# Steps 13 to 17 of a tuned linear-attention and MLP kernel in three batches, with earlier casts and reordered transfers

## Chip, cores, metric

One core of a Trainium2 chip. The metric is the device time of one execution in microseconds (us); lower is better. A ratio is the mean time of one kernel's runs over that of the other's of the same rounds, so it is not quite the ratio of the medians quoted beside it; the interval given with it is a 95% interval.

## The reference

A block-wise linear attention with decay (4 batches, 8 heads, 768 positions, head dimension 64) is followed by a two-layer MLP with a tanh-GELU (512 to 2048 to 512, no bias) on its 3072 output rows. Cut to what matters:

```python
for b in range(nb):                                   # blocks of 64 positions
    intra = (qb @ kb^T * Dmask) @ vb                  # Dmask: lam ** (i - j), causal
    out[:, :, sl] = intra + (qb * lam_pow) @ kv_state
    kv_state = lam_block * kv_state + (kb * rev_pow)^T @ vb
x = out.transpose(0, 2, 1, 3).reshape(B * S, H * D)
return gelu_tanh(x @ w_in) @ w_out
```

## The kernel before

The attention is cut into 24 steps (256 positions of 4 heads each). A step needs q, k and v loaded, cast to fp16 with their decay (q on VectorE, k on ScalarE, v on GpSimd), q and k transposed by DMA, and then, on TensorE, scores S, products with v (O or OK), state updates K, and products of the old state u. On VectorE PT is the masked S, and t the state; on GpSimd u is the state with its mask. The finished rows x of two steps feed the MLP. Its dense matmuls stand in a queue of pieces, `filler`, and `fill(n)` issues n of them between the attention's steps, so that TensorE always has work. Some pieces carry sums on VectorE behind them (`gs`; the MLP's second product is done with seven block products in place of eight).

```python
def prep_v(s):                                        # v of step s, on GpSimd
    tv = a16p.tile([P, 2, HH, D], FP16, tag="v16", name=f"v16_{s}")
    pin(nc.gpsimd.tensor_tensor(wide(tv[:]), ld32[s][2][:], decay(dv, s), ALU.mult))
    a16[s] = a16[s] + (tv,)
    ...                                               # loads of step s + 3 are issued here

def R(n, s, ahead=None):                              # one step: S of n, products of s
    scores(n); ...; products(n, s); causal(n)         # causal: PT = S * mask, on VectorE
    ...; update(n, 0)                                 # t on VectorE, u on GpSimd

def burst(ns, ss, *mix):                              # a batch: S of all ns, then O of ss, K of ns, u
    for n in ns: scores(n)
    ...
    for n in ns: causal(n)
    ...
    for n in ns: update(n, 0)

# which sums stand behind which piece (groups of 512 rows)
behind(9, 0, 4, (1, 2, 4, 3))                         # first halves, behind piece 9 of 16
for k, m in zip(..., (1, 2, 4, 3)):
    behind(n1 + k, 4, 8, (m,))                        # second halves

FILL = {8: (0, 2, 1, 2), ..., 12: (0, 2, 1, 3),
        13: (0, 2, 1, 3), 14: (0, 3, 1, 3), 15: (0, 2, 1, 3), 16: (0, 2, 1, 3), 17: (0, 3, 1, 3)}
for n, (a, b, c, d) in FILL.items():                  # one step at a time
    stage_t(n); fill(a)
    prep_qk(n + 2) if n == 8 else prep(n + 2)
    fill(b); R(n, n - 1); fill(c); U(n)               # U: second half of the update
    ...
burst((18, 19), (17,))                                # from here on: two at a time
```

All matmuls write to one pool of eight PSUM buffers, called banks here; a tile waits until the earlier tile of its bank has been read. `pin` keeps the program's order on each engine.

## Time and profile before

| | before |
|---|---|
| time, median of 3 runs | 199.89 us (199.67 to 200.28) |
| profiled span | 198.3 us |
| busy share PE / DVE / ACT / POOL | 97% / 77% / 62% / 37% |
| PE, 87.21 to 119.52 us (the stretch that is rewritten) | busy throughout |

PE is TensorE, DVE VectorE, ACT ScalarE, POOL GpSimd, SPq the queue that issues transfers. A line of a timeline has start and duration in us, engine, line of the source, operation, output and inputs, shapes, the number of like instructions in a row, and in brackets the idle time before it with what ended it. The lines of the kernel before that carry the argument stand in the prediction below.

### The profile page before, as it was taken

To read this page: it belongs to the slowest core of one execution; us is meant where nothing else is said; L and a number is where in the kernel's file an instruction comes from. 1 tells how busy PE (TensorE), PEld (TensorE's weight loads), DVE (VectorE), ACT (ScalarE), POOL (GpSimd) and SP (SyncE) were. 2 spreads that over 40 slices of the span, in tenths; PEclk is the share of its full clock that TensorE was granted. 3 is DMA by queue.
4 is the path that set the end of the run, shared out by engine and by line. 5 is a ranking of instruction groups with operands and counts; after the bars stand their busy time and mean duration, and the time that the engine had idled before them with its cause. 6 is when DMAs were issued, how large, how long until landed. Compare 5 with 4: busy or idle time off the path is not lost.

```text
span 198.3 us, 5936 instructions
## 1 busy us (share of the span) xinstructions
PE 191.9 (97%) x2437; PEld 139.7 (70%) x2439; DVE 151.8 (77%) x296; ACT 123.0 (62%) x251; POOL 73.6 (37%) x85
## 2 busy tenths in 40 slices
PE   8879999999999999999999999999999999999993
PEld 2546544456887888754588755578888888888883
DVE  4887722789989989949899378999678997588720
ACT  3673878466693675577745486754668835778321
POOL 6594223456456652436433565047002030002000
PEclk9999999999999999999999999999999999999999
DMA  6999999999999999999864999320211200020205
GB/s 171 291 324 386 386 386 387 292 289 295 293 297 257 217 293 215 210 317 219 226 142 104 271 286 214 106 56 0 53 37 72 105 9 0 0 108 1 106 3 212
DMA packets 61706, 37.86 MB, mean 191 GB/s; under 512 B 17520, under 2 KB 54640, under 8 KB 61680
## 3 DMA queue, kind: packets, MB, share of 16 engines
q1 hardware_dynamic: 61136, 37.23, 71.8%
q8 instruction: 19, 0.31, 0.7%
q10 hardware_dynamic: 544, 0.26, 0.5%
q14 instruction: 7, 0.06, 0.1%
HBM read 27.26 MB, written 6.29 MB: 169 GB/s over the span
## 4 chain that ended last, share of the span: by engine, by line
PE 88%; SPq 4%; DMA 4%; ACT 1%; issue 1%
PE Hps L529 24%; PE MX L606 17%; PE MY L606 9%; PE HX L698 7%; PE O2ps L544 7%; PE MW L606 4%; DMA wi<-in_moe_w_in_dram 4%; SPq L70 4%; PE HY L698 4%; PE S L327 3%; PE Hps L789 3%; PE OK L385 2%; PE HW L698 2%; PE OK L376 2%; PE Tps L298 1%; PE O L436 1%
## 5 line engine op out<-in xcount | busy, mean ns | idle before, releaser
L529 PE MATMUL Hps<-xT,w_in 128*128 128x512 f16 (+1 forms) x288 | 51.0, 332 | 0.0
L488 POOL TENSOR_TENSOR u<-t,lumask 128x256 f16<-128x256 f32 x40 | 29.6, 752 | 49.7 <-DVE t L481 34.1
L529 PEld LDWEIGHTS <-w_in 128*128 128x128 f16 x288 | 27.8, 98 | 18.8
L533 ACT ACTIVATE gT<-Hps 128x512 f16<-128x512 f32 x56 | 32.9, 597 | 10.3 <-PE Hps L529 9.8
L337 DVE TENSOR_TENSOR PT<-S,mask 128x512 f16<-128x512 f32 x48 | 30.5, 682 | 7.4 <-PE S L327 7.3
L606 PEld LDWEIGHTS <-gs 128*128 128x128 f16 x320 | 31.1, 98 | 4.0 <-DVE gs L576 0.4
L258 POOL TENSOR_TENSOR v<-v,dv 128x512 f16<-128x512 f32 x24 | 29.9, 1249 | 7.3 <-DMA v<-in_v_dram 6.9
L606 PEld LDWEIGHTS <-gT 128*128 128x128 f16 x240 | 23.2, 98 | 3.5 <-ACT gT L533 0.5
L606 PE MATMUL MX<-w_sum,gs 128*128 128x256 f16 x160 | 21.5, 273 | 0.0
L271 DVE TENSOR_TENSOR qk<-q,dq 128x512 f16<-128x512 f32 x23 | 19.1, 835 | 1.1 <-DMA q<-in_q_dram 1.0
L576 DVE TENSOR_TENSOR gs<-gT 128x1024 f16<-128x1024 f16 (+1 forms) x24 | 18.4, 772 | 1.6 <-ACT gT L533 1.6
L276 ACT ACTIVATE qk<-k 128x512 f16<-128x512 f32 x24 | 15.0, 626 | 6.9 <-DMA k<-in_k_dram 6.7
L651 POOL TENSOR_TENSOR o<-u,q 128x512 f32<-128x512 f32 (+1 forms) x5 | 5.4, 1082 | 37.2 <-ACT u L623 37.2
L462 ACT ACTIVATE xT<-OK 128x256 f16<-128x256 f32 x34 | 13.0, 454 | 6.3 <-PE OK L385 6.0
L544 PE MATMUL O2ps<-w_out,gT 128*128 128x512 f16 x64 | 14.6, 379 | 0.0
L698 PEld LDWEIGHTS <-ws 128*128 128x128 f16 x128 | 12.5, 98 | 1.8
L623 ACT ACTIVATE u<-MX 128x256 f32<-128x256 f32 x18 | 6.9, 384 | 10.1 <-PE MX L606 10.1
L481 DVE SCALAR_TENSOR_TENSOR t<-t,lamu,OK 128x64 f32<-128x64 f32 x48 | 11.0, 274 | 1.4 <-issue 0.5
L327 PEld LDWEIGHTS <-qkT 64*64 64x64 f16 x384 | 6.1, 106 | 7.1 <-issue 3.4
L544 PEld LDWEIGHTS <-gT 128*128 128x128 f16 x64 | 6.1, 98 | 6.6
L606 PE MATMUL MY<-w_out,gs 128*128 128x256 f16 x80 | 10.7, 273 | 0.0
L606 PE MATMUL MX<-w_sum,gT 128*128 128x256 f16 x80 | 10.4, 273 | 0.0
(95 smaller groups left out, 311.6 us busy)
## 6 DMA issues: line engine op xcount, KB each, us to landing
q<-in_q_dram SPq DMA_DIRECT2D x24, 256.0 KB, 5.0
k<-in_k_dram SPq DMA_DIRECT2D x24, 256.0 KB, 5.1
v<-in_v_dram SPq DMA_DIRECT2D x23, 256.0 KB, 5.4
out_dram<-o SPq DMA_DIRECT2D x17, 256.0 KB, 4.1
wo<-in_moe_w_out_dram SPq DMA_DIRECT2D x4, 1024.0 KB, 9.5
wi<-in_moe_w_in_dram SPq DMA_DIRECT2D x4, 512.0 KB, 8.0
wi<-in_moe_w_in_dram SPq DMA_DIRECT2D x2, 1024.0 KB, 12.7
out_dram<-o SPq DMA_DIRECT2D x3, 512.0 KB, 5.0
```

What stands on the lines that cost most here:

```text
L258: pin(nc.gpsimd.tensor_tensor(wide(tv[:]), ld32[s][2][:], decay(dv, s), ALU.mult))
L271: pin(q_eng.tensor_tensor(wide(tq), q32[:], decay(dq, s), ALU.mult))
L276: pin(nc.scalar.activation(out=wide(tk), in_=k32[:], func=AF.Copy))
L337: pin(nc.vector.tensor_tensor(t[:, hl].rearrange("p b c d -> p b (c d)"), Sps[:].rearrange("p b c d -> p b (c d)"), mask[:].unsqueeze(1).t ...
L462: pin(nc.scalar.activation(out=d, in_=o, func=AF.Copy))
L488: pin(nc.gpsimd.tensor_tensor(u[:], state[half][:].unsqueeze(2).to_broadcast([P, 2, 2, D]), lumask[:, 2 * half : 2 * half + 2, :].unsqueez ...
L529: pin(nc.tensor.matmul(by_block(Hps[:, i, :]), w_in16[:, c, f * P : (f + 1) * P], x(c), start=(c == 0), stop=(c == NC - 1)))
L533: pin(nc.scalar.activation(out=dst, in_=Hps[:], func=AF.Gelu_apprx_tanh))
L544: pin(nc.tensor.matmul(O2[tau][0][:], gT[:, f % HF, f // HF, tau * P : (tau + 1) * P], w_out16[:, f, :], start=(n == 0), stop=(n == NF - 1)))
L576: pin(nc.vector.tensor_tensor(g_rows(m, i), g_rows(a, i), g_rows(b, i), op))
L606: pin(nc.tensor.matmul(dst, lhsT, rhs, start=(opens and i == 0), stop=(closes and i == HF - 1), skip_group_check=True))
L698: pin(nc.tensor.matmul(dst[:, i, :], w_in_block(a, slice(c, c + 1), slice(f * P, f * P + P))[:, 0], x_block(b, slice(c, c + 1))[:, 0], sta ...
```

## The change

Intent: handle steps 13 and 14, and 15 and 16, as batches (step 17 stays alone), so that the small matmuls stand together more often, and take the casts and transfers that a batch needs early enough. By the words of its author: "Steps 13 to 17 in three batches; casts of 15 and 16 two and three products ahead, loads of 18 behind the transposition of 16".

```diff
-                whole = g == 3 or (g, T) == (4, 0)      # store of group 4 in one transfer
+                whole = g == 3
...
+        if n == 12:
+            prep_qk(15)
         fill(d)
...
+    cast_qk(16)
+    fill(2)
+    burst((13, 14), (12,))
+    transpose_dma(16)
+    fill(1)
+    U(13)
+    U(14)
+    prep_v(15)                 # with the loads of 18
+    prep_v(16)                 # with the loads of 19
+    fill(6)
+    burst((15, 16), (13, 14))
+    fill(1)
+    U(15)
+    U(16)
+    prep(17)
+    fill(8)
+    prep(18)
+    R(17, 15)
...                            # prep 19 to 21 and the w_in sums, between pieces
-    burst((18, 19), (17,))
+    burst((18, 19), (16, 17))
+    prep_v(21)
```

Cuts: the removed rows 13 to 17 of `FILL`, the split of `prep_qk` into `cast_qk` and `transpose_dma`, and a condition that keeps a batch closing an even step from queueing its group too soon.

More of the change, by code (lines that the diff above doesn't have):

```diff
@@ L266, in prep_qk, with cast_qk @@
     def prep_qk(s):
+        cast_qk(s)
+        transpose_dma(s)
+    def cast_qk(s):
         q32, k32, _ = ld32[s]
@@ L277, in prep_qk, with transpose_dma @@
         a16[s] = (tq, tk)
+        whole_qk[s] = tqk
+    whole_qk = {}
+    def transpose_dma(s):
+        tqk = whole_qk.pop(s)
         if s >= FIRST_DMA_T:
@@ L444, in burst @@
         g, i = group_of[sbg]
-        if i == len(groups[g]) - 1:
+        if ss[-1] % 2 == 1 and i == len(groups[g]) - 1:
             queue_group(g, *mix)
@@ L971 @@
     fill(2)
-    FILL = {8: (0, 2, 1, 2), 9: (2, 2, 1, 2), 10: (0, 1, 1, 3), 11: (0, 2, 1, 2), 12: (0, 2, 1, 3),
-            13: (0, 2, 1, 3), 14: (0, 3, 1, 3), 15: (0, 2, 1, 3), 16: (0, 2, 1, 3), 17: (0, 3, 1, 3)}
+    FILL = {8: (0, 2, 1, 2), 9: (2, 2, 1, 2), 10: (0, 1, 1, 3), 11: (0, 2, 1, 2), 12: (0, 2, 1, 3)}
     for n, (a, b, c, d) in FILL.items():
@@ L984 @@
             prep_v(n + 2)
-        if n == 17:
-            prep_qk(20)
-            fill(1)
-            prep_qk(21)
-            fill(1)
-            prep_v(20)
-            prep_v(21)
-            fill(1)
-        else:
-            fill(d)
-        if 8 < n < 17:
-            sum_win((n - 7) // 2, (n - 1) % 2, nc.vector)
-    burst((18, 19), (17,))
+        if n == 12:
+            prep_qk(15)
+        fill(d)
+        if n > 8:
+            sum_win((n - 7) // 2, (n - 1) % 2, nc.vector)
+    cast_qk(16)
[16 more added lines that the diff above has]
+    R(17, 15)
+    fill(1)
+    U(17)
+    fill(1)
+    sum_win(3, 0, nc.vector)
+    fill(2)
+    prep(19)
+    sum_win(3, 1, nc.vector)
+    fill(2)
+    sum_win(4, 0, nc.vector)
+    fill(2)
+    sum_win(4, 1, nc.vector)
+    fill(2)
+    prep_qk(20)
+    fill(1)
+    prep_qk(21)
+    prep_v(20)
+    fill(3)
+    burst((18, 19), (16, 17))
+    prep_v(21)
     fill(2)
```

## The prediction

> **What bounds the kernel now.** I read the page first, then the chain of waits, then the waits of TensorE alone, then the timelines of PE, DVE and POOL between 80 and 130 us, where the changed steps lie.
>
> ```profile
> PE 191.9 (97%) x2437; PEld 139.7 (70%) x2439; DVE 151.8 (77%) x296; ACT 123.0 (62%) x251; POOL 73.6 (37%) x85
> PE 88%; SPq 4%; DMA 4%; ACT 1%; issue 1%
> ```
>
> TensorE is busy for 97% of the span, and the chain that ended last is PE for 88%; the rest is the load at the start and the last store. The list of waits, cut to PE and to 86 to 127 us, is empty, and the window 87.21 to 119.52 us has PE busy 32.31 of 32.31 us. So in the stretch that is rewritten nothing is waited for: only the issue time of the matmuls counts, and the change can win only by making the small matmuls cheaper, or lose by making PE wait. How dear the small matmuls are shows in the PE timeline:
>
> ```profile
> 87.21 0.42 PE L327 MATMUL S<-qkT 64*64 64x128 f16 x16
> 87.91 0.28 PE L385 MATMUL OK<-qkT,u 128*128 128x128 f16 x2
> 88.03 6.21 PE L529 MATMUL Hps<-xT,w_in 128*128 128x512 f16 x28
> ...
> 118.15 0.64 PE L327 MATMUL S<-qkT 64*64 64x128 f16 x32
> 119.28 0.40 PE L436 MATMUL O<-qkT,u 128*128 128x128 f16 x4
> 119.52 7.07 PE L529 MATMUL Hps<-xT,w_in 128*128 128x512 f16 x32
> 126.52 0.64 PE L327 MATMUL S<-qkT 64*64 64x128 f16 x32
> 127.81 0.40 PE L436 MATMUL O<-qkT,u 128*128 128x128 f16 x4
> 128.05 2.75 PE L529 MATMUL Hps<-xT,w_in 128*128 128x512 f16 x12
> ```
>
> From the first S to the next dense matmul, a single step takes 0.82 us (87.21 to 88.03; two matmuls of u) or 0.93 us (four of u); a batch of two steps that closes one takes 1.37 us (118.15 to 119.52), and one that closes two 1.53 us (126.52 to 128.05). Dense pieces of four 128x512 matmuls take 0.875 us each (eight in 119.52 to 126.52).
>
> The second thing to see is how DVE and POOL hold each other up:
>
> ```profile
> 103.55 0.68 DVE L636 TENSOR_TENSOR o<-MW,m 128x512 f32<-128x512 f32 x1
> 104.15 0.79 DVE L576 TENSOR_TENSOR gs<-gT 128x1024 f16<-128x1024 f16 x1
> 104.86 1.53 DVE L151 TENSOR_TENSOR ws<-w_in,ws 128x1024 f16<-128x1024 f16 x1
> ```
> ```profile
> 104.35 1.49 POOL L258 TENSOR_TENSOR v<-v,dv 128x512 f16<-128x512 f32 x1
> 112.86 1.04 POOL L258 TENSOR_TENSOR v<-v,dv 128x512 f16<-128x512 f32 x1
> ```
> ```profile
> 122.94 0.74 DVE L576 TENSOR_TENSOR gs<-gT 128x1024 f16<-128x1024 f16 x1 [0.68 <-ACT gT L533]
> 123.71 0.98 DVE L576 TENSOR_TENSOR gs<-gs,gT 128x1024 f16<-128x1024 f16 x1
> ```
>
> A v product alone takes 1.04 us, a ws or gs sum alone 0.68. Beside each other they take turns: gs ends at 104.94; v, issued at 104.35, ends at 105.84, 0.90 after it; ws, issued at 104.86, ends at 106.39, 0.55 after v. PT and t, with one input from SBUF, are not held.
>
> **What the Trainium skill says.** "SBUF — State Buffer", section "SBUF: two separate sides": the port pair that VectorE and GpSimd share is an exclusive lock, taken by a GpSimd operation or by a VectorE operation with two SBUF inputs; the other blocks for the whole instruction. The trace agrees, with the 0.90 and 0.55 us above. "TensorE: Matmul & The Clock Gate", section "Part 3: Packing small matmuls — row/col tiling": matmuls on different tiles overlap, and all complete in order. The trace agrees with the first (32 S matmuls of 216 ns span 0.64 us), and the second is why a held matmul holds all PE work. "Perfetto Trace Analysis", section "Identifying the Most-Contended Engine", warns that matmul busy time is no measure of headroom; so I use start-to-start times, not the 97%.
>
> **The change part by part.**
>
> 1. *PE, saved.* The order of instructions shows the same 4870 PE rows. Before, the stretch holds steps 13 and 14 (0.82 each), 15, 16, 17 (0.94, 0.93, 0.93) and the batch of 18 and 19 (1.37): 5.81 us. After, it holds a batch 13+14 that closes 12: 1.37 less two u matmuls at 0.058 = 1.26; a batch 15+16 that closes 13 and 14: 1.53 plus two u (0.11) less 8 missing K matmuls (0.06) = 1.58; step 17 alone 0.93; the batch 18+19 that closes 16 and 17: 1.53 + four u (0.24) = 1.77. Sum 5.54, so 0.27 us less. Between groups and dense work each group also loses an overlap: the dense matmuls of the stretch, 64 of 216 ns and 112 of 109 ns, make 26.04 us, but 32.31 - 5.81 = 26.50 us pass, 0.077 per group of six. Two groups fewer save 0.15. Together **0.42 us**.
>
> 2. *Casts and transpositions.* The casts of 15 and 16 move to ACT and DVE time that was idle (DVE waits 2.43 us before 87.67). The transposition of 16 is queued when 12 is closed, about 88.5 us, and right behind that of 15, which landed at 92.4 before (86.73 + 5.66). The loads of 18 no longer stand between the two. It should land near 93.3; PE wants it at 94.9. No wait, no gain.
>
> 3. *The store of group 4* becomes two transfers instead of one, near 140 us; the queue is idle there. Nothing.
>
> 4. *DVE and POOL behind the first batch.* This is where I expect a new wait. Call the batch's first S time B = 87.21. The first batch of the kernel before is the template, with B = 118.15: four PT end at B+2.95, u products start at B+3.22 and end at B+3.84, 4.41, 4.98, and gs 1 is issued at B+4.8 (here 4.7: fewer u matmuls), once gelu 8 is done. Now POOL has v of 15 and v of 16 queued straight behind the four u. Taking turns: gs 1 behind u 3, B+5.53; u 4, B+6.00; gs 2, B+6.54; v15 B+7.44; gs 3 B+7.99; v16 B+8.89; gs 4 B+9.44. Only then come the PT of step 15 in DVE's order: B+9.36 to B+10.05. PE gets to the batch 15+16 after 1.26 + 7 x 0.875 = B+7.39, needs v16 at about B+8.43 (waits to 8.9), and would start the next dense matmul at 7.39 + 1.58 = B+8.97. But that one writes the PSUM bank which S of step 15 held: in the built program, its wait on DVE is 15 counts behind that of the first dense piece after batch 13+14, and these 15 end at the first PT of step 15. So PE waits to about B+10.1: **1.13 us lost**, the wait for v16 included in it.
>
> 5. *Behind that.* The transposition of 17 is issued near 101.3 and lands 3.1 us later (as the one at 99.78 did), 104.4; S of 17 comes at 105.1. Later batches: DVE's queue behind 18+19 has one v more (21), some 0.6 us; PT of 20 then meets its S just in time. No loss.
>
> Sum: 199.89 - 0.42 + 1.13 = 200.60.
>
> **Rivals.**
> - *A: no new wait, the saving alone: 199.5.* For it: the moves of casts and loads look made to keep PE fed, and had gs 1 been issued 0.3 us earlier (before u 3) one turn would fall before v16, and PT of 15 would be in time. Against: gs 1 waited for gelu in the template too, and that follows PE's own pace to 0.1 us.
> - *B: the wait is shorter, 0.3 to 0.7 us: 199.8 to 200.2.* It needs v16 or a sum to go out of turn. The trace shows no such case.
> - *C: a transposition late as well.* The one of 16 has 1.6 us of room, that of 17 has 0.7. If DMA is slower (6.5 us to landing, the longest in the view of qkT), S of 17 waits 2 to 3 us more, 202 to 203. The queue is nearly empty near 101 us, so I give it little.
> - *D: PE busy time falls by more, since batches have fewer switches.* The 1.37 and 1.53 us of existing batches bound that: no more than 0.1 us beyond part 1.
>
> **Range and chances.** I give the wait of part 4 two chances in three, A and B nearly all the rest. The sum is 200.6; weighed with A and B I name **200.4 us**, range **199.3 to 201.0**. The runs before scatter from 199.67 to 200.28, so the sign itself is near the noise. 2% is 4 us, far from any of these: faster 0.005, within 2% 0.985, slower 0.01.
>
> **What would show it.** Right: in the profile after, batches of about 1.26, 1.6 and 1.77 us where PE doesn't wait; gs sums lengthened to 1.0 to 1.5 us beside v of 15 and 16; the first PT of step 15 some 2 us behind its S; and on PE one gap near 1.1 us before the first dense matmul behind batch 15+16, put down to DVE PT, with a shorter one at the K matmuls put down to POOL v. Wrong: no gap of PE in 94 to 99 us (then A, near 199.5); a gap at S of 16 or 17 put down to a transposition (C); batch times far from these (part 1).

## The result, and the profile after

201.09 us median (200.69 to 201.81, six runs) against 199.88 us (199.67 to 200.28, six runs): ratio 1.0063, interval 1.0037 to 1.0089. Slower, but by less than 2%, and 0.09 us above the predicted range. The six times stand in two groups: 200.69, 200.70, 200.74, and 201.43, 201.74, 201.81. The profiled run, 201.74, is of the upper group.

From the page of the changed kernel (lines of the steps stand 10 higher than before; L337 is now S, L347 PT, L586 gs, L539 Hps; v stays at L258):

```profile
PE 191.9 (96%) x2437; PEld 140.2 (70%) x2439; DVE 153.9 (77%) x296; ACT 122.7 (61%) x251; POOL 74.9 (37%) x85
PE 77%; DMA 8%; DVE 6%; SPq 4%; ACT 3%; issue 1%; DVEq 0%; ACTq 0%
```

PE is as busy as before to the tenth, and the span grew from 198.3 to 199.9 us, so the difference appears as waiting (only roughly: the ends of matmuls are modelled). The chain now runs over DVE and a transfer as well. The waits of PE from 60 us on, which were none before:

```profile
PE MX L616 <- ACT gT L543: 0.8, 1, 0.8
PE Hps L539 <- DVE PT L347: 0.4, 1, 0.4
PE K L435 <- POOL v L258: 0.3, 1, 0.3
```

The second and third are the ones foretold. The timeline of PE through them:

```profile
88.05 0.64 PE L337 MATMUL S<-qkT 64*64 64x128 f16 x32
89.30 6.21 PE L539 MATMUL Hps<-xT,w_in 128*128 128x512 f16 x28
95.44 0.64 PE L337 MATMUL S<-qkT 64*64 64x128 f16 x32
...
97.00 0.31 PE L435 MATMUL K<-v,qk 64*64 64x64 f16 x8 [0.35 <-POOL v L258]
97.24 0.51 PE L446 MATMUL O<-qkT,u 128*128 128x128 f16 x6
98.15 3.61 PE L539 MATMUL Hps<-xT,w_in 128*128 128x512 f16 x16 [0.40 <-DVE PT L347]
```

With B = 88.05 (B is the first S of step 13), K of step 16 waits to B+8.95 (foretold 8.9) and the dense matmul to B+10.10 (foretold about 10.1). The two idle times in brackets make only 0.75 us, but from its first S to the dense matmul the batch takes 2.71 us, 1.10 more than the 1.61 us that it takes below without waits. Start-to-start times are the ones to go by. DVE and POOL in the same time:

```profile
92.72 0.85 DVE L586 TENSOR_TENSOR gs<-gT 128x1024 f16<-128x1024 f16 x1 [0.38 <-ACT gT L543]
93.61 0.99 DVE L586 TENSOR_TENSOR gs<-gs,gT 128x1024 f16<-128x1024 f16 x1
94.63 1.42 DVE L586 TENSOR_TENSOR gs<-gT,gs 128x1024 f16<-128x1024 f16 x1
95.97 1.53 DVE L586 TENSOR_TENSOR gs<-gT 128x1024 f16<-128x1024 f16 x1
97.42 2.47 DVE L347 TENSOR_TENSOR PT<-S,mask 128x512 f16<-128x512 f32 x4
```
```profile
91.27 2.77 POOL L498 TENSOR_TENSOR u<-t,lumask 128x256 f16<-128x256 f32 x4 [5.74 <-DVE t L488]
94.01 2.94 POOL L258 TENSOR_TENSOR v<-v,dv 128x512 f16<-128x512 f32 x2
```

The four sums take 0.85 to 1.53 us each, where one alone takes 0.68, and the two v products 2.94 us together, where one alone takes 1.04. They take turns, and the first PT of step 15 starts at B+9.37 (foretold 9.36), almost two us behind its S at B+7.39. Seen alone it takes 0.68 us, to 98.10, and the dense matmul that was waiting for it starts at 98.15.

The first wait in the list was not foretold. It lies at 60.85 us, far ahead of the change:

```profile
58.09 0.63 ACT L280 ACTIVATE qk<-k 128x512 f16<-128x512 f32 x1 [1.00 <-DMA k<-in_k_dram]
```
```profile
60.85 0.28 PE L616 MATMUL MX<-w_out,gT 128*128 128x256 f16 x1 [0.81 <-ACT gT L543]
```

A cast of k on ACT waited 1.00 us for its load, the gelus behind it came late, and PE waited for them. In the kernel before the same cast did not wait:

```profile
56.98 0.63 ACT L276 ACTIVATE qk<-k 128x512 f16<-128x512 f32 x1
```

Before the casts and transfers of step 15, the two programs are the same on every engine. The traces show the same instructions in the same order; addresses, which traces do not show, I compared in the programs. Nothing of the change that I can find would put this wait there, and the runs below support that: two further profiles of the changed kernel do not have it, and a second profile of the kernel before does.

Where the 1.6 us of the profiled runs lie, from the starts of S in the timelines of PE and the spans:

| us | before | after |
|---|---|---|
| start to S of 8 | 57.25 | 57.27 |
| S of 8 to S of 9 (shared part) | 7.34 | 8.16 |
| S of 9 to S of 13 | 22.62 | 22.62 |
| S of 13 to the dense matmul behind batch 18+19 | 32.31 | 32.94 |
| from there to S of 20 | 7.00 | 7.00 |
| S of 20 to the end | 71.78 | 71.88 |

### The profile page after: what moved, and what is told of

Its sections match the earlier page's. It is cut to its first block, busy times and chain, and to the rows that moved or that the text cites. A ratio compares the mean times of both kernels' runs of the same rounds, so it can differ in the third digit from the quotient of the medians.

```text
span 199.9 us, 5931 instructions
## 1 busy us (share of the span) xinstructions
PE 191.9 (96%) x2437; PEld 140.2 (70%) x2439; DVE 153.9 (77%) x296; ACT 122.7 (61%) x251; POOL 74.9 (37%) x85
## 4 chain that ended last, share of the span: by engine, by line
PE 77%; DMA 8%; DVE 6%; SPq 4%; ACT 3%; issue 1%; DVEq 0%; ACTq 0%
PE Hps L539 19%; PE MX L616 17%; PE MY L616 9%; PE HX L708 7%; PE O2ps L554 6%; PE MW L616 4%; DMA wi<-in_moe_w_in_dram 4%; SPq L70 4%; PE HY L708 4%; DMA k<-in_k_dram 3%; PE Hps L799 3%; PE S L337 2%; DVE gs L586 2%; PE HW L708 2%; DVE PT L347 2%; ACT gT L543 1%
## 5 line engine op out<-in xcount | busy, mean ns | idle before, releaser
L539 PE MATMUL Hps<-xT,w_in 128*128 128x512 f16 (+1 forms) x288 | 50.8, 332 | 0.4 <-DVE PT L347 0.4
L498 POOL TENSOR_TENSOR u<-t,lumask 128x256 f16<-128x256 f32 x40 | 30.2, 769 | 49.6 <-DVE t L491 28.8
L539 PEld LDWEIGHTS <-w_in 128*128 128x128 f16 x288 | 27.8, 98 | 19.6 <-issue 0.5
L347 DVE TENSOR_TENSOR PT<-S,mask 128x512 f16<-128x512 f32 x48 | 30.3, 680 | 5.9 <-PE S L337 5.9
L258 POOL TENSOR_TENSOR v<-v,dv 128x512 f16<-128x512 f32 x24 | 30.3, 1267 | 7.9 <-DMA v<-in_v_dram 7.6
L586 DVE TENSOR_TENSOR gs<-gT 128x1024 f16<-128x1024 f16 (+1 forms) x24 | 17.0, 714 | 2.7 <-ACT gT L543 2.7
L472 ACT ACTIVATE xT<-OK 128x256 f16<-128x256 f32 x26 | 9.9, 454 | 7.3 <-PE OK L395 7.3
L472 ACT ACTIVATE xT<-O 128x256 f16<-128x256 f32 x22 | 8.0, 459 | 6.4 <-PE O L446 5.6
L616 PE MATMUL MX<-w_out,gT 128*128 128x256 f16 x80 | 10.2, 273 | 0.9 <-ACT gT L543 0.8
L586 DVE TENSOR_TENSOR gs<-gs,gT 128x1024 f16<-128x1024 f16 (+1 forms) x12 | 10.6, 887 | 0.3
```

What stands on the lines that cost most here:

```text
L347: pin(nc.vector.tensor_tensor(t[:, hl].rearrange("p b c d -> p b (c d)"), Sps[:].rearrange("p b c d -> p b (c d)"), mask[:].unsqueeze(1).t ...
L472: pin(nc.scalar.activation(out=d, in_=o, func=AF.Copy))
L498: pin(nc.gpsimd.tensor_tensor(u[:], state[half][:].unsqueeze(2).to_broadcast([P, 2, 2, D]), lumask[:, 2 * half : 2 * half + 2, :].unsqueez ...
L539: pin(nc.tensor.matmul(by_block(Hps[:, i, :]), w_in16[:, c, f * P : (f + 1) * P], x(c), start=(c == 0), stop=(c == NC - 1)))
L586: pin(nc.vector.tensor_tensor(g_rows(m, i), g_rows(a, i), g_rows(b, i), op))
L616: pin(nc.tensor.matmul(dst, lhsT, rhs, start=(opens and i == 0), stop=(closes and i == HF - 1), skip_group_check=True))
```

## The experiments

Theory: the batches save PE 0.42 us, and the turns that gs sums and v products take cost it 1.13 us. Rivals: batches cost more than they look; v of 16 alone holds PE; transfers hold it. A second question came from the result: is the upper group of times a mark of the change (C2), or of a load that either kernel meets by chance (C1)? Kernels are compared only within the same rounds.

| run | median us (kernel) | median us (before) | ratio, interval | S13 to dense, us |
|---|---|---|---|---|
| e1_before_again | 200.05 | 199.96 | 1.0000, 0.9969 to 1.0030 | 32.31 |
| e1_after_again | 200.70 | 199.96 | 1.0030, 1.0005 to 1.0054 | 32.94 |
| e2_v_early | 199.67 | 199.96 | 0.9978, 0.9952 to 1.0003 | 31.85 |
| e3_two_sums_late | 200.27 | 199.96 | 1.0009, 0.9973 to 1.0044 | 31.93 |
| e4_before_k7_late | 199.87 | 199.85 | 0.9994, 0.9977 to 1.0011 | 32.31 |
| e4_best | 199.71 | 199.85 | 0.9995, 0.9974 to 1.0016 | 31.85 |
| e5_loads_first | 201.94 | 199.85 | 1.0123, 1.0079 to 1.0167 | 33.53 |
| e6_casts_late | 199.56 | 199.85 | 0.9988, 0.9965 to 1.0010 | 31.85 |
| e7_after_third | 200.71 | 199.84 | 1.0039, 1.0023 to 1.0056 | 32.94 |
| e7_after_k7_late | 200.72 | 199.84 | 1.0050, 1.0029 to 1.0071 | 32.93 |
| e7_v_early_again | 199.66 | 199.84 | 0.9989, 0.9969 to 1.0009 | 31.85 |
| e7_old_store | 199.42 | 199.84 | 0.9978, 0.9953 to 1.0002 | 31.85 |
| e8_before_k10_late | 200.32 | 200.10 | 1.0015, 0.9993 to 1.0037 | 32.31 |
| e8_after_k10_late | 200.74 | 200.10 | 1.0044, 1.0025 to 1.0064 | 32.93 |
| e8_best | 199.46 | 200.10 | 0.9967, 0.9953 to 0.9981 | 31.85 |

The last column, from the first S of step 13 to the dense matmul behind batch 18+19, comes out of one profile each and repeats to 0.01 us over profiles that share that stretch; the whole times of one run spread over 0.35 to 2.6 us. That makes it the sharper instrument for what the change did.

### The two kernels again

No edit.

> A control: the kernel before, word for word, timed against itself. All theories: ratio 1.000 within noise (interval about 0.997 to 1.003). It also shows how often the late load in the part that both kernels share (steps 5 to 8) costs time: the changed kernel's profile lost 0.84 us there, before step 13, although its instructions, addresses and waits are the same as before's up to that point, and its six times fell into two groups, near 200.7 and near 201.6. Theory C1 (chance of the loads, in either kernel): here too some of the runs are 0.6 to 1.0 us above the others. Theory C2 (the changed kernel is hit more often): these runs stay within 0.6 us of each other, 199.7 to 200.3.

> The changed kernel again. Main theory (0.42 us saved, 1.1 us lost at the first dense matmul behind batch 15+16): the runs that are not hit by the late load come out at 200.6 to 200.8 again, 0.6 to 0.9 us above before, and the distance from the first S of step 13 to the first dense matmul behind batch 18+19 is 32.9 us (before: 32.3). C1: the group near 201.6 is seen less often or as often as by chance, and in the control too. C2: again about half of the runs near 201.6.

> The changed kernel a third time, for its scatter and one more profile. Its first six times had three of 201.4 to 201.8, its second six one of 201.2, the others lie at 200.5 to 200.8. C1 (the late load hits either kernel by chance, about one run in six, as it did before: 4 of 34 runs over 0.6 us above the lowest group): none to two of six over 201.2, median 200.6 to 200.8. C2 (the changed kernel is hit more often): two to four of six over 201.2. In an unhit profile the first S of 13 to that of 20 takes 39.9 us again (before: 39.3).

Measured: the control gave 199.8 to 200.94, one of six 0.55 us above the next; the kernel before, run 11 times beside it, had two such (200.92 and 201.28). The changed kernel gave 200.54 to 201.16, then 200.59 to 200.99. The unchanged changed kernel ran 18 times: four were above 201.1, three of them in the first six. The kernel before ran 56 times, control included: five were above 200.5. (Counted alike, as times more than 0.6 us above the kernel's own median, it is three of 18 against five of 56.) So upper times belong to either kernel; C1's main point holds. The control's profile shows the cause at work in the kernel before: the same cast waits 0.8 us for k, PE 0.3 us for the gelu behind it, and S of 8 to S of 9 takes 7.53 us. For the profiled high run of the changed kernel this load is nearly the whole story: its span is 1.16 us longer than that of e7_after_third, and 1.03 us of this lie between S of 8 and S of 9 (8.16 against 7.13). Whether the changed kernel meets such times somewhat more often these counts do not decide: of its times above 201.1, three of six fell in the first call and one of twelve after it. The median of the 18 is 200.74 us.

### Moving what takes turns

> Changed kernel, but the v products of 15 and 16 stand on POOL ahead of the first batch, where it idles for 5.7 us; the loads of 18 and 19 stay where the change put them. Main theory (gs sums and v products take turns, so PT of 15 comes late): the sums end near B+7.0 (B: first S of step 13), PT of 15 starts within 0.6 us of its S, both waits of PE behind batch 15+16 vanish, 1.1 us less than the changed kernel, 0.3 to 0.5 us less than before: ratio to before 0.998 (unhit runs near 199.5). Rival (batches of two cost PE more than the profile of before tells, or ACT or DMA is the cause): PE still waits or the distance B to the dense matmul behind batch 18+19 stays over 32.5 us, ratio 1.003 or more.

> The changed kernel with v of 15 and 16 early, a second time: median 199.5 to 199.7, ratio to before 0.998 (first: 0.9978, 0.9952 to 1.0003), first S of 13 to that of 20 38.8 us. If the first result was luck: 0.999 or more.

```diff
+    def cast_v(s): ...             # the product alone
+    def load_behind(s): ...        # the loads of s + 3 alone
     cast_qk(16)
+    cast_v(15)
+    cast_v(16)
     fill(2)
     burst((13, 14), (12,))
...
-    prep_v(15)
-    prep_v(16)
+    load_behind(15)
+    load_behind(16)
```

```profile
93.41 0.69 DVE L592 TENSOR_TENSOR gs<-gT,gs 128x1024 f16<-128x1024 f16 x1
94.02 0.68 DVE L592 TENSOR_TENSOR gs<-gT 128x1024 f16<-128x1024 f16 x1
94.68 2.48 DVE L353 TENSOR_TENSOR PT<-S,mask 128x512 f16<-128x512 f32 x4
```
```profile
84.28 2.94 POOL L262 TENSOR_TENSOR v<-v,dv 128x512 f16<-128x512 f32 x2
90.05 2.77 POOL L504 TENSOR_TENSOR u<-t,lumask 128x256 f16<-128x256 f32 x4 [2.84 <-DVE t L494]
```
```profile
94.22 0.64 PE L343 MATMUL S<-qkT 64*64 64x128 f16 x32
95.48 0.51 PE L452 MATMUL O<-qkT,u 128*128 128x128 f16 x6
95.83 2.54 PE L545 MATMUL Hps<-xT,w_in 128*128 128x512 f16 x11
```

These are the timelines of DVE, POOL and PE. (In this kernel lines stand another 4 to 6 higher.) The v products now run at 84 us, behind step 12. The last two sums take 0.69 and 0.68 us, their time alone, and PT of 15 starts 0.46 us behind its S, as early as S lets it. PE has no wait at all from 60 us on, and the batch 15+16 takes 1.61 us (94.22 to 95.83; foretold 1.58). The stretch takes 31.85 us: 1.09 less than in the changed kernel (foretold 1.1) and 0.46 less than before (foretold 0.42). The sums end at B+7.87 (B is 86.83 here), not at the B+7.0 that I expected, because they still take turns with u; that is just in time. In time the gain over the kernel before is small: 0.9978 and 0.9989, and neither interval excludes 1.

> Changed kernel with its POOL order, but two of the four gs sums of the first half are put behind the cast of 17, so that PT of 15 and 16 stand in front of them on DVE. Main theory: v of 15 and 16 then meet at most one sum, v16 is ready near B+8.5 (PE wants it at B+8.4) and PT of 15 starts by B+7.9; PE's wait for PT vanishes, the one for v16 shrinks to 0.1 us or none; ratio to before 0.998 to 0.999. Rival (v16 alone holds PE, the sums do not matter): PE still waits 0.35 us for v16, ratio 1.003 or more. A new wait at MY, for the later sums, is possible on both.

```diff
-            behind(9, 0, 4, (1, 2, 4, 3))
+            if g == 3:
+                behind(9, 0, 4, (1, 2))
+                behind(13, 0, 4, (4, 3))
+            else:
+                behind(9, 0, 4, (1, 2, 4, 3))
```

Here POOL keeps the order of the changed kernel, and two sums step back on DVE, whose timeline shows:

```profile
92.70 0.98 DVE L586 TENSOR_TENSOR gs<-gs,gT 128x1024 f16<-128x1024 f16 x1
94.99 2.48 DVE L347 TENSOR_TENSOR PT<-S,mask 128x512 f16<-128x512 f32 x4 [1.31 <-PE S L337]
99.14 0.69 DVE L586 TENSOR_TENSOR gs<-gT,gs 128x1024 f16<-128x1024 f16 x1
```

DVE now idles 1.31 us ahead of PT instead of coming late to it. The v products, 2.94 us in the changed kernel, take 2.48 us, and PE waits neither for v nor for PT. The stretch takes 31.93 us. So the rival that v of 16 alone holds PE falls: the same v products, in the same place behind the four u, are in time once the sums are out of their way. Its ratio, 1.0009, missed my 0.998 to 0.999: three of its six times were 200.7 to 201.5, the other three 199.49 to 199.85. Its one profile, of a low time, does not show why.

### The transfers and the casts

> The kernel with v of 15 and 16 early (the batches without waits), but the loads of 18 again ahead of the transposition of 16 on the queue. If that part of the change matters: the transposition of 16 lands some 2.7 us later (three loads of about 0.9 us each between 15 and 16), near B+8.8 instead of B+6.1 (B: first S of 13), PE wants it at B+7.6: a wait of about 1.2 us at S of 16, ratio to before 1.003 to 1.005, about 1.2 us over the same kernel with the loads behind. If the transfer is hidden anyway: no wait at S of 16, ratio 0.998.

> The kernel with v of 15 and 16 early, but the casts of q and k of 15 and 16 right ahead of batch 13+14 instead of two and three pieces before it. If the early casts matter: the transposition of 15 is issued 1 to 2 us later, that of 16 lands after PE wants it (B+7.6) and S of 15 or 16 waits; or PT of 13 waits for the casts on DVE. Ratio 1.001 or more. If not: the transposition of 15 still lands near B+5.5 and that of 16 near B+6.5, no wait of PE, ratio 0.998 as with the casts early.

Both are edits of the kernel with v early; in the second the two v products move back by the same two pieces:

```diff
# e5_loads_first                          # e6_casts_late
+    load_behind(15)                      -        if n == 12:
     burst((13, 14), (12,))               -            prep_qk(15)
     transpose_dma(16)                    +    fill(2)
...                                       +    prep_qk(15)
-    load_behind(15)                            cast_qk(16)
     load_behind(16)                            ...
                                          -    fill(2)
                                                burst((13, 14), (12,))
```

With the loads of 18 first, the queue and a wait of PE read:

```profile
86.36 2.02 SPq L296 DMA_TRANSPOSE qkT<-qk  x1
...
89.94 1.50 SPq L70 DMA_DIRECT2D v<-in_v_dram  x1
91.61 1.64 SPq L296 DMA_TRANSPOSE qkT<-qk  x1
```
```profile
97.24 0.42 PE L343 MATMUL S<-qkT 64*64 64x128 f16 x16 [1.49 <-DMA qkT<-qk]
```

The transposition of 16 is issued behind three loads, at 91.61 us, and S of 16 waits 1.49 us for it (foretold about 1.2); the stretch takes 33.53 us, 1.68 more than with the loads behind. So the batches need this part of the change. (In the kernel before, the single step 16 has its S at 106.55 us, 19 us behind S of 13 and not 8; that it would not need the order is argued, not run.) The ratio, 1.0123, is beyond the 1.003 to 1.005 expected: the stretch alone loses more than the 1.2 us, its profile loses another 0.70 us between S of 4 and S of 8, and one of four times was 204.23, which no trace explains.

The early casts, in contrast, buy nothing: with the casts late the stretch takes 31.85 us, to the hundredth what it takes with them early, and PE waits for nothing. With B at 86.88, the transpositions of 15 and 16 are then issued 1.25 and 2.6 us after the batch's first S, and both still land before PE wants them:

```profile
88.13 2.75 SPq L296 DMA_TRANSPOSE qkT<-qk  x2
```

### The store

> The same kernel (v early) with the first store of group 4 in one transfer again, as before the change. Expected by all theories: nothing, ratio within 0.001 of the run with v early, last S to end of the span as there.

```diff
-                whole = g == 3
+                whole = g == 3 or (g, T) == (4, 0)
```

From S of 20 to the end of the span it takes 71.77 us; all eleven profiles that split this store take 71.86 to 71.89, and the profiles of the kernel before 71.76 to 71.79. The last run below, whose store is whole as well, takes 71.78 us. So the split costs 0.1 us, at the very end of the program and not where the store stands. PE's last product comes at the same distance from S of 20 in the profiles before and after; the 0.1 us lie behind it. What makes them I did not trace.

### The scatter of the shared part

> The kernel before, with the casts and the v product of step 7 moved from ahead of two dense pieces to behind the products of step 5. Of the runs so far, those that are 0.6 to 1.5 us above their fellows (before: 200.9, 201.3; the changed kernel: 201.4 to 201.8; the one with two late sums: 200.7 to 201.5) are put down to the load of k of step 7: ACT waits for it ahead of two gelus that PE needs for S of 9 (S of 8 to S of 9: 7.34 us in the profile of before, 8.16 in that of the changed kernel, 7.1 to 7.5 in the others). Theory: moved, the gelus no longer stand behind the load; S of 8 to S of 9 is 7.1 us whatever the load does, all runs lie within 0.4 us, median 199.6 to 199.8, ratio 0.997 to 0.999. Rival (the wait only moves on, to the transposition of 7 on PE): as scattered as before, ratio 1.000 or more.

> Both mends together: v products of 15 and 16 early, and the casts of 7 late. Theory: the gains add: 0.47 us in the stretch of the batches (measured with v early) and what the kernel before gains from the casts of 7; runs within 0.4 us, median 199.2 to 199.5, ratio to before 0.996. Rival: the casts of 7 bring a wait of their own; ratio 0.998 or more.

> The changed kernel with the casts of step 7 behind the products of step 5. If the load of k of step 7 is what splits its times: six runs within 0.4 us, 200.5 to 200.8, ratio 1.003 to 1.004. If it is one of several late loads: one or two runs are still 0.5 us or more above the rest (as two of six were with v early and the casts of 7 late: 200.2 and 200.6 over 199.6).

```diff
     U(5)
-    prep(7)
     sum_wout(1, 3, DVE)
     fill(2)
     R(6, 5)
+    prep(7)
```

These three were aimed at the wrong step. The traces name a tile, not its step; I counted the casts of k wrongly and took the late one for that of step 7. Counted along the program's order it is that of step 10, whose load the v product of step 7 issues, so the edit even made that load later. The kernel before gave 199.66 to 200.01, no high time in six; but with v early two of six stood 0.4 us or more above the rest, and the changed kernel had two of 201.5, with S of 8 to S of 9 at 8.09 us in its profile and the 0.8 us wait of PE for a gelu again. They say nothing for the theory they were to test.

> The kernel before with the casts of q and k of step 10 behind the products of step 7 instead of ahead of two dense pieces. A correction first: the runs with the casts of step 7 late were aimed at the wrong step. In program order the cast that waits in the profile of the changed kernel (58.09 us, 1.00 us behind the load) is that of step 10, and its load is issued by the v product of 7, which those runs moved back too. Theory: with the gelus ahead of this cast no run is hit: six within 0.4 us, S of 8 to S of 9 7.1 us, median 199.6 to 199.8, ratio 0.998. Rival (hits come from other loads): one run or more 0.6 us above the rest.

> The changed kernel with the same move. Theory: all six runs at 200.4 to 200.8, none at 201.2 or above; first S of 13 to that of 20 39.9 us, as the stretch of the batches is not touched; ratio 1.003 to 1.004. Rival: hits remain, so the spread of the first six times has another cause.

> v of 15 and 16 early, the store of group 4 whole as before, and the casts of 10 late: all six runs at 199.2 to 199.6, ratio to before 0.997, with an interval that excludes 1.000. Rival: as scattered as the others, 0.998 to 0.999.

```diff
-        prep_qk(n + 2) if n == 8 else prep(n + 2)
+        if n > 8:
+            prep(n + 2)
         fill(b)
         R(n, n - 1)
+        if n == 8:
+            prep_qk(n + 2)
```

With the casts of step 10 out of the way the 0.8 us wait of PE is in none of the three profiles (S of 8 to S of 9: 7.27, 7.16 and 7.45 us). That proves little: without this move it is in only two of 14 profiles, and most of the others have 7.13 to 7.20 us, no more than here. And the scatter stays: the kernel before gave 199.64 to 201.14, and one of the changed kernel's six was 201.89. So this load is one source of high times, as the traces in which PE waits behind it show, and not the only one; that the move removes it is not shown. The profile of the first of the three loses time before S of 4 (41.84 us, 41.3 to 41.6 in all others). Which loads make the other high times stays open: only one time of each run has a trace.

The last run combines v early, the store whole, and the casts of 10 late. Its five times are 199.25 to 199.79 us against a median of 200.10 for the kernel before: ratio 0.9967, interval 0.9953 to 0.9981. It is the only version whose interval lies wholly below 1. In the traces its sure part is the 0.46 us of the stretch; the rest may be the lot of that call, in which the kernel before was 0.1 to 0.3 us slower than in the others.

## Why the prediction was right or wrong

By its own steps:

- **The saving on PE (0.42 us): right.** The batches took 1.25, 1.61 and 1.73 us where nothing held them, and step 17 0.93, as in the timelines of PE: 5.52 us in all against 5.54 foretold. The stretch without waits is 0.46 us shorter than before.
- **Casts and transpositions, "No wait, no gain": right** for the kernel as it stands. The runs split it further: putting the loads behind the transposition saves a wait of 1.49 us that a batch would otherwise bring; the early casts save nothing (with v early; with v late this was not run). When the transposition of 16 landed no trace tells; it is only seen that PE did not wait for it.
- **The store, "Nothing": wrong by 0.1 us**, in the tail, as the run with the store whole showed.
- **DVE and POOL behind the first batch (1.13 us): right in mechanism and size.** PE waited to B+10.10, the sums and products ended within 0.02 us of the foretold times, and moving either side away took 1.09 and 1.01 us off the stretch. (That PT is not held was stated there without a number: in the kernel before two PT at 81.51 us took 1.27 us beside a GpSimd product, and two at 87.67 us, beside none, 1.29.)
- **Behind that, "No loss": right.** S of 17, 18 and 20 wait for nothing.
- **Rivals:** A (no wait) and B (a shorter one) fall with the trace. C, a late transposition, did not happen, but e5_loads_first shows that one change of order on the queue makes it happen. D had put no more than 0.1 us beyond the 0.42; 0.04 was there.
- **The step that failed: the part of the program ahead of step 13, which the sum leaves out and the range covers only by its last words,** "The runs before scatter from 199.67 to 200.28, so the sign itself is near the noise." I took three times of the kernel before for its whole scatter. What the runs showed in its place: the load of k of step 10 lands 5.5 us after its issue in one profile and 7.0 in another, ACT waits 1.00 us for it, PE 0.81 us behind that, and S of 8 to S of 9 takes 8.16 us in place of 7.34 (7.13 in most profiles). Whole times 0.7 to 1.4 us above a kernel's median come in both kernels, five in 56 before and three in 18 after. In the two high runs that were profiled (201.74, and 201.57 with the casts of 7 late) the trace puts them down to this load; for the other high runs the cause stays open. All three of the 18 fell into the six on record and lifted their median from about 200.7 to 201.09. By the counts that may well be bad luck, but a range for a median of six had to leave room for it; its top, 201.0, lay 0.4 us above the sum.
- **Two smaller errors.** Having worked out 200.60, I named 200.4, giving a third of the weight to rivals that the trace spoke against. And the sum was closer by some luck: the stretch lost 0.63 us where I had 0.71, the store 0.1 where I had nothing, and the two nearly cancel. The median of all 18, 200.74, still lies 0.14 above 200.60.

## What to carry to other kernels

When an engine off the critical path gets a longer run of work at once, ask which buffers it will release late: here two GpSimd products in a row made VectorE's sums late, the sums made a mask late, and the mask held a PSUM bank that TensorE wanted. The same two products, moved into idle time some eight microseconds earlier, turned a loss of 0.63 us in the stretch into a gain of 0.46. And where a gain of some tenths of a microsecond is at stake, measure the distance between two marks in the trace as well as the whole time: the distance repeated to 0.01 us, while the times of one unchanged kernel scattered by up to 1.6 us.

## What the Trainium skill lacked or had wrong

- "SBUF — State Buffer", section "SBUF: two separate sides": the exclusive lock fits what these traces show. The page lacks how long a blocked operation still takes once the lock comes free: here less than its time alone (a sum of 0.68 us ended 0.55 us after the GpSimd product that held it, a v product of 1.04 us ended 0.90 us after the sum; why is not shown). It also lacks who comes next when both engines have work queued: here they took strict turns, over all of the four sums and the products beside them.
- The cost of going between small tiles and dense matmuls has no figure on any page that I read; it would belong to "TensorEngine Tiling (Array Packing)", section "Key Properties". As an estimate from the timelines here it is 0.077 us per group before (26.50 less 26.04 us over six groups) and 0.073 in the kernel without waits (31.85 less 5.52 less 26.04, over four).
- No page that I read says how far a load's landing varies from run to run of a fixed program: the load of k of step 10 took 5.5 us in the profile before and 7.0 in that after, with the same instructions in front of it.
